# First batch of a fused attention and MLP kernel: K and Q loaded six tokens a row on 96 partitions, strided reads of PSUM, plain key layout, first loads on other queues, the bias table loaded and turned by head pair

## The chip, the cores and the metric

The kernel runs on one core of one Trainium2 chip. The metric is device time in microseconds (us), lower is better. Every experiment ran beside the kernel before on the same chip in the same rounds.

How ratios are computed: a ratio is the mean time of one kernel's runs over the mean time of the runs of the kernel before of the same rounds, with a 95% interval. So it is not quite the ratio of the medians that are quoted beside it.

Engines in the text: PE is TensorE, ACT is ScalarE, DVE is VectorE, POOL is GpSimd, SP is SyncE.

## The reference, cut to what matters

```python
# q, k, v: (8 batches, 8 heads, 576 tokens, 64);  bias_table: (32 buckets, 8 heads)
scores = scale * np.matmul(q, k.transpose(0, 1, 3, 2))
rel = pos[:, None] - pos[None, :]
bucket = ...                                  # a function of |rel|, 32 buckets; far ones are all bucket 31
scores = scores + bias_table[bucket].transpose(2, 0, 1)[None]
attn = exp(scores - max); attn = attn / (sum + 1e-09)
x = (attn @ v)  ->  (4608 tokens, 512)
h = x @ w_in                                  # 512 x 2048
s = np.sin(alpha * h)
out = (h + s * s / (alpha + 1e-09)) @ w_out   # 2048 x 512
```

## The kernel before

The program interleaves batches: while batch t goes through its MLP, the attention of batch t+1 fills the gaps of PE. From about 70 us on that works so well that PE is never free. What is left to gain is the ramp: batch 0's attention, whose K and Q have to be loaded, transposed and copied, and whose position bias has to be built first.

**Scheduling.** A small list scheduler in the program (`plan`) decides at build time on which engine, and in which order, the tasks of PE, ACT and DVE go, from rough durations and from constants such as `T_M2` (the earliest time that it assumes for the bias multiplications). POOL's part, the loads and the bias chain stand in plain program order ahead of it. On the chip each engine then runs its own list strictly in order.

**The bias.** `exp(score + bias)` is computed as `exp(score) * exp(bias)`. The small table `exp(bias)` (8 heads by 512 distances) is made by one matmul (`e_sb`), written to HBM (`e_dram`), read back as 128 shifted rows a head (`m2r`), and turned end for end by POOL (`m2`). For the last 64 keys POOL makes a second form, `mh`, from two slices of `m2`. DVE multiplies bands of the exponentials by `m2` or `mh` before PE multiplies them with V.

```python
    for p in range(NP):                               # NP = 4 pairs of heads
        nc.gpsimd.tensor_copy(
            out=m2[:, 2 * p : 2 * p + 2, :], in_=m2r[:, 2 * p : 2 * p + 2, ::-1]
        )
    me = m2.rearrange("p (hp two) x -> p two hp x", two=2)
    nc.gpsimd.tensor_copy(out=mh[0:64, :, :], in_=me[0:64, 0, :, 0:192])
    nc.gpsimd.tensor_copy(out=mh[64:128, :, :], in_=me[64:128, 1, :, 64:256])
    cast_v(nc.gpsimd, 0)                              # V of batch 0: f32 -> f16, 6 casts
    load_w_in16()                                     # 4 loads, issued by POOL
    for kq, src in ((0, k), (1, q)):
        load_nat(nat2, kq, 0, H, src[1], nc.gpsimd)   # K and Q of batch 1
```

**K and Q of a batch.** Tokens are loaded two to a row (512 bytes), in three loads each, transposed by PE and copied out of PSUM by ACT or DVE. The keys of the odd head are stored with their last 64 ahead of the other 512, which takes an extra small copy.

```python
    SI = 2
    SN = (128, 128, 32)
    SO = (0, 256, 512)
    ...
    def load_nat(dst, kq, h0, h1, src, eng, parts=(0, 1, 2)):
        for j in parts:
            n, o = SN[j], SO[j]
            eng.dma_start(
                out=dst[0:n, j, kq],
                in_=src[h0:h1, o : o + SI * n].rearrange("h (p i) d -> p h (i d)", i=SI),
            )
    ...
        eng = {"DVE": 0.75, "ACT": 0.7}               # the copies: the scheduler may choose
        return [plan.add(eng, cp(x), [m], pri, use=[b]) for x in range(1 if kq else 2)]
```

**Pairs.** Batch 0's attention is done in four pairs of heads (0 to 3), each in two windows of queries (384 and 192). A window ends with an `Ln` on ACT (the softmax denominator's reciprocal is taken as exp(-ln)). So "pair 0's second Ln" marks the end of pair 0's work, and its time is a good mile mark. In a window's order on DVE the multiplication by `mh` belongs to the second window:

```python
                def bh(e):
                    io = u.v[:, 8, 384:576]
                    nc.vector.tensor_tensor(out=io, in0=io, in1=mh[:, p, 0:192], op=ALU.mult)

                x = plan.add({"DVE": 0.17}, bh, [x] + mh_tasks, base + 10, nb=band_nb, use=[ub])
```

The softmax here doesn't subtract the row's maximum and nothing guards it: scores larger than these inputs give would overflow.

## Time and profile before

| | before |
|---|---|
| time, median of 3 runs | 446.3 us (446.24 to 446.53) |
| PE busy, of a span of 445.2 us | 426.2 us (96%) |
| ACT, DVE, POOL busy | 385.3, 261.9, 91.0 us |
| PE busy in the first 50 us | 38.7 us |
| PE busy from 70 to 440 us | 368.0 of 370 us |
| first exp of batch 0 on ACT | 14.70 us |
| pair 0's second Ln | 27.02 us |
| first matmul with w_in (batch 0's MLP begins) | 49.81 us |

PE is idle for 19.0 us of the whole span (445.2 less 426.2), and nearly all of that lies before 70 us or at the very end. So a gain should show as an earlier first matmul with w_in, with everything behind it shifted as a block. (The runs x1, x2 and x10 will show that this mile mark and the time go together only to within 1 to 2 us. The prediction below has 39.7 where the stretches of the trace add up to 38.7; nothing rests on it.)

The table of stretches of the kernel before. Columns: stretch and its length, then busy time (and number of instructions) of PE, weight loads, DVE, ACT, POOL, then PE's mean granted clock (1.00 is full), the busy share of the DMA engines, GB/s.

```profile
core 0: us, PE busy (x) PEld busy (x) DVE busy (x) ACT busy (x) POOL busy (x), PEclk, DMA share, GB/s
15.00:20.00 5.00, 4.60 (x68) 2.92 (x66) 4.49 (x8) 3.57 (x10) 3.67 (x5) 1.00 1.06 239
20.00:25.00 5.00, 2.75 (x41) 1.77 (x38) 3.64 (x7) 4.45 (x12) 4.83 (x9) 1.00 0.31 70
25.00:30.00 5.00, 4.55 (x54) 2.95 (x56) 2.69 (x8) 3.47 (x10) 5.00 (x9) 1.00 1.05 209
30.00:35.00 5.00, 4.70 (x66) 3.57 (x66) 2.25 (x7) 4.97 (x15) 1.22 (x2) 1.00 1.07 205
```

From 30 us ACT is full (4.97 of 5): from there ACT's exponentials set the pace. Before that none of PE, DVE and ACT is full; POOL is, from 20 to 30 us (4.83 and 5.00), and waits set the pace. POOL's timeline of the kernel before says which. Columns: start, duration, engine, line, operation, written and read tile, shapes, count; in brackets the idle time ahead of it and what ended it. (`m2r` shares its memory with `w_out`, so `w_out_80<-e_dram` is the load of `m2r`; `m_77` is `m2`.)

```profile
16.27 3.32 POOL L454 COPY m_77<-w_out_80 128x768 f16<-128x768 f16 x4 [5.81 <-DMA w_out_80<-e_dram]
19.65 1.03 POOL L458 COPY mh<-m_77 64x768 f16<-64x768 f16 x1
20.72 0.93 POOL L459 COPY mh<-m_77 64x768 f16<-64x768 f16 x1
21.71 2.44 POOL L354 CAST v_71<-w_out_80 128x512 f16<-128x512 f32 x4
24.11 0.92 POOL L356 CAST vh_73<-w_out_80 64x256 f16<-64x256 f32 x2
24.98 2.14 POOL L372 DMA_DIRECT2D w_in_79<-in_moe_w_in_dram  x4
```

POOL starts when `m2r` lands (16.27), turns all four pairs, makes all of `mh`, and only then casts V. PE has to wait for that last piece. PE's timeline of the kernel before, the two waits that matter:

```profile
24.61 0.82 PE L388 MATMUL av<-u,vh_73 128*64 128x384 f16 x2 [2.20 <-POOL vh_73 L356]
...
47.81 0.60 PE L501 MATMUL mo<-id_sb,nat_95 128*64 128x128 f16 x8 [1.00 <-DMA nat_95<-in_q_dram]
```

So PE waits 2.20 us for the V cast in pair 0, and 1.00 us for batch 1's Q just before the MLP can begin. ACT's timeline of the kernel before gives the mile marks (first exp; pair 0's second Ln; pair 3's first Ln; the load of the sine table, where ACT turns to the MLP):

```profile
14.70 1.61 ACT L580 ACTIVATE u<-sc 128x384 f16<-128x384 f32 x4
...
27.02 0.33 ACT L662 ACTIVATE lnd<-av 128x192 f32<-128x192 f32 x1 [0.25 <-PE av L646]
...
44.95 0.65 ACT L662 ACTIVATE lnd<-av 128x384 f32<-128x384 f32 x1
...
47.53 1.28 ACT L771 ACT_TABLE_LOAD   x1
```

### The profile page before, as it was taken

The page shows a single profiled execution, that of the slowest core. Times are in us where ns is not written, and L with a number is a line of the kernel's source. Part 1 is how long each engine was busy: PE and PEld are TensorE (multiplying, and loading weights), DVE is VectorE, ACT ScalarE, POOL GpSimd, SP SyncE. Part 2 cuts the span into 40 slices and gives each one's busy share as a digit, 9 for nine tenths or more (in the row PEclk, how much of TensorE's full clock was granted, in tenths as well). Part 3 has the DMA queues.
Part 4 walks back from the last instruction along what each step waited for, and adds up shares of the span by engine and source line. Part 5 has one row for each costly group of instructions (what it writes and reads, how often), then busy time and mean ns, then how long its engine had stood idle before and what let it go on. Part 6 is the DMA issues. An engine that isn't in the chain of part 4 may idle for free.

```text
span 445.2 us, 12071 instructions
## 1 busy us (share of the span) xinstructions
PE 426.2 (96%) x4940; PEld 302.8 (68%) x4940; DVE 261.9 (59%) x555; ACT 385.3 (87%) x844; POOL 91.0 (20%) x104
## 2 busy tenths in 40 slices
PE   5879999999999999999999999999999999999996
PEld 1555545876688668866886688558876787666663
DVE  3646786548655865577457755785568555907400
ACT  2789889999999999999999999999999999936511
POOL 8578931016000700080008000400000000000000
PEclk9999999999999999999999999999999999999999
DMA  9699999909913990099529900981000000011111
GB/s 139 179 183 195 175 168 157 187 29 146 190 38 79 142 151 24 26 127 176 90 37 161 167 31 27 110 138 40 1 26 25 25 26 26 1 49 47 49 72 71
DMA packets 144950, 41.51 MB, mean 93 GB/s; under 512 B 132424, under 2 KB 139776, under 8 KB 144896
## 3 DMA queue, kind: packets, MB, share of 16 engines
q0 software_dynamic: 94720, 16.88, 47.9%
q1 hardware_dynamic: 49360, 23.52, 25.2%
q8 instruction: 38, 0.62, 0.6%
q10 hardware_dynamic: 816, 0.36, 0.4%
q14 instruction: 16, 0.13, 0.1%
HBM read 37.56 MB, written 16.52 MB: 121 GB/s over the span
## 4 chain that ended last, share of the span: by engine, by line
PE 72%; DMA 10%; ACT 10%; DVE 2%; issue 2%; POOL 2%; SPq 1%; ACTq 0%; POOLq 0%; DVEq 0%
PE sc L388 32%; PE mo L388 25%; PE av L646 12%; PE av L388 3%; DMA nat_95<-in_q_dram 3%; DMA w_in_79<-in_moe_w_in_dram 2%; DMA qT_69<-staged_q 2%; ACT L771 2%; ACT sq L716 2%; DVE g L723 1%; DMA w_out_80<-e_dram 1%; DMA tabL<-in_bias_table_dram 1%; POOL m_77 L454 1%; DMA e_dram<-e_sb 1%; ACT u L580 1%
## 5 line engine op out<-in xcount | busy, mean ns | idle before, releaser
L580 ACT ACTIVATE u<-sc 128x384 f16<-128x384 f32 x448 | 175.1, 535 | 1.4 <-PE sc L388 1.3
L388 PE MATMUL mo<-w_out_80,g 128*64 128x512 f16 x1152 | 172.1, 379 | 0.0
L388 PE MATMUL sc<-xT,w_in_79 128*64 128x512 f16 x1152 | 132.6, 379 | 1.0 <-DVE g L723 1.0
L613 DVE TENSOR_TENSOR u<-u,m_77 128x512 f16<-128x512 f16 (+1 forms) x192 | 73.9, 402 | 81.1 <-ACT u L580 81.0
L723 DVE SCALAR_TENSOR_TENSOR g<-sq,inv_a,sc 128x512 f16<-128x512 f16 x144 | 102.2, 744 | 23.9 <-PE mo L388 12.3
L388 PEld LDWEIGHTS <-w_in_79 128*64 128x64 f16 x1152 | 78.0, 110 | 45.4 <-DVE g L723 2.0
L388 PEld LDWEIGHTS <-g 128*64 128x64 f16 x1152 | 79.3, 110 | 22.0
L388 PE MATMUL sc<-qT_70,kz_67 128*64 128x384 f16 (+1 forms) x576 | 68.0, 287 | 2.0 <-ACT u L580 1.1
L388 PE MATMUL sc<-qT_69,kz_66 128*64 128x384 f16 (+1 forms) x576 | 67.1, 292 | 2.3 <-ACT u L580 1.3
L388 PEld LDWEIGHTS <-kz_67 128*64 128x64 f16 x576 | 43.0, 108 | 20.5 <-issue 5.3
L388 PEld LDWEIGHTS <-kz_66 128*64 128x64 f16 x576 | 40.6, 109 | 20.6 <-issue 9.3
L646 PE MATMUL av<-u,ones 128*64 128x192 f16 (+1 forms) x512 | 43.9, 286 | 0.0
L677 DVE TENSOR_TENSOR xT<-av,rd 128x384 f16<-128x384 f32 (+1 forms) x68 | 29.4, 437 | 24.1 <-ACT rd L666 19.9
L479 ACT ACTIVATE outs<-mo 128x512 f32<-128x512 f32 x15 | 8.9, 595 | 30.7 <-PE mo L388 30.7
L646 PEld LDWEIGHTS <-ones 128*64 128x64 f16 x512 | 30.5, 110 | 4.2
L662 ACT ACTIVATE lnd<-av 128x384 f32<-128x384 f32 x64 | 29.3, 458 | 3.4 <-PE av L646 2.9
L335 POOL DMA_DIRECT2D v_72<-in_v_dram x12 | 10.6, 897 | 101.7 <-PE av L646 101.7
L666 ACT ACTIVATE rd<-lnd 128x384 f32<-128x384 f32 x64 | 28.8, 449 | 1.4
L335 POOL DMA_DIRECT2D v_71<-in_v_dram x12 | 11.7, 1215 | 73.0 <-PE av L646 73.0
L646 PE MATMUL av<-u,v_71 128*64 128x384 f16 (+1 forms) x256 | 22.1, 286 | 0.0
L646 PE MATMUL av<-u,v_72 128*64 128x384 f16 (+1 forms) x256 | 21.8, 286 | 0.0
L388 PE MATMUL av<-u,ones_76 128*64 128x192 f16 (+1 forms) x128 | 20.4, 286 | 0.0
(360 smaller groups left out, 413.0 us busy)
## 6 DMA issues: line engine op xcount, KB each, us to landing
out_dram<-outs SPq DMA_DIRECT2D x36, 256.0 KB, 2.0
staged_k<-in_k_dram POOLq DMA_DIRECT2D x6, 576.0 KB, 13.0
staged_q<-in_q_dram POOLq DMA_DIRECT2D x6, 576.0 KB, 17.7
w_out_80<-in_v_dram SPq DMA_DIRECT2D x8, 256.0 KB, 4.9
w_in_79<-in_moe_w_in_dram POOLq DMA_DIRECT2D x4, 512.0 KB, 11.1
w_out_80<-in_moe_w_out_dram POOLq DMA_DIRECT2D x4, 512.0 KB, 9.1
v_71<-in_v_dram POOLq DMA_DIRECT2D x12, 128.0 KB, 7.2
v_72<-in_v_dram POOLq DMA_DIRECT2D x12, 128.0 KB, 7.5
```

The costliest lines, as they stand in the source:

```text
L335: nc.gpsimd.dma_start(out=vs[t % 2][:, c], in_=vp[128 * c : 128 * c + 128],)
L388: nc.tensor.matmul(out=out[64 * z : 64 * z + 64], lhsT=lhsT[:, 64 * z : 64 * z + 64], rhs=rhs, start=start, stop=stop,)
L479: nc.scalar.activation(out=o, in_=i, func=AF.Copy)
L580: nc.scalar.activation(out=u.v[:, k0 : k0 + nc_, q0 : q0 + n], in_=sc.v[:, 0 : n * nc_], func=AF.Exp, scale=0.125,)
L613: nc.vector.tensor_tensor(out=io, in0=io, in1=m2[:, 2 * p : 2 * p + 2, x0 : x0 + hi - lo], op=ALU.mult,)
L646: nc.tensor.matmul(out=o[64 * z : 64 * z + 64, 0:n], lhsT=vs[t % 2][:, c, 2 * p + z, :] if y else ones, rhs=u.v[:, 4 * z + c, q0 : q0 + n] ...
L662: nc.scalar.activation(out=ln.v[:, 0:n], in_=avs[0].v[:, 0:n], func=AF.Ln)
L666: nc.scalar.activation(out=rd.v[:, 0:n], in_=ln.v[:, 0:n], func=AF.Exp, scale=-1.0)
L677: nc.vector.tensor_tensor(out=xT[:, p, (x0 + a) % XN : (x0 + a) % XN + m - a], in0=avs[1].v[:, a:m], in1=rd.v[:, a:m], op=ALU.mult,)
L716: nc.scalar.activation(out=sq.v, in_=s16.v, func=AF.Square)
L723: nc.vector.scalar_tensor_tensor(out=gcell[b].v[:, f, :], in0=sq.v, scalar=inv_a[:, f : f + 1], in1=h.v, op0=ALU.mult, op1=ALU.add,)
L771: nc.scalar.preload_act_table_set(name)
```

## The change

Its intent is to start batch 0 sooner: larger rows in the first loads and fewer of them, no long run of warm-up matmuls ahead of the first transposes, and a bias chain that delivers pair 0's part first. The parts of the diff that matter (cut; `...` marks cuts):

```diff
-T_M2 = 13.0
+T_M2 = 11.0
...
-WARM1 = 6
+WARM1 = 1
...
-    SI = 2
-    SN = (128, 128, 32)
+    SI = 6
+    SN = S // SI                      # 96
...
-    load_nat(nat0, 0, 0, 2, k[0], nc.sync)
+    load_nat(nat0[:, 0], 0, 2, k[0], nc.sync)
     nc.sync.dma_start(out=tabN, in_=bias_table)
...
+    load_nat(nat0[:, 1], 0, 2, q[0], nc.scalar)
+    nc.scalar.dma_start(out=tabL, ...)
...
+    load_v32(0, nc.sync)              # before: behind the load of m2r
...
-    nc.vector.tensor_copy(out=e_sb, in_=eps_[0:H, 0:EW])
-    nc.sync.dma_start(out=e_dram.ap(), in_=e_sb)
+    nc.scalar.activation(out=e_sb, in_=eps_[0:H, 0:EW], func=AF.Copy)
+    nc.scalar.dma_start(out=e_dram.ap(), in_=e_sb)
...
-    nc.sync.dma_start(out=m2r, ...)   # all 8 heads
...
-    for p in range(NP):
-        (reverse pair p of m2r into m2)
+    load_m2r(0, 2)                    # pair 0 alone, issued by POOL
+    for kq, src in ((0, k), (1, q)):
+        load_nat(nat1[:, kq, 2:6], 4, H, src[0], nc.gpsimd)
+    load_m2r(2, H)
+    turn(0)                           # reverse pair 0
+    cast_v(nc.gpsimd, 0)
+    load_w_in16()
+    for p in range(1, NP):
+        turn(p)
     me = m2.rearrange("p (hp two) x -> p two hp x", two=2)
     nc.gpsimd.tensor_copy(out=mh[0:64, :, :], in_=me[0:64, 0, :, 0:192])
     nc.gpsimd.tensor_copy(out=mh[64:128, :, :], in_=me[64:128, 1, :, 64:256])
-    cast_v(nc.gpsimd, 0)
-    load_w_in16()
...
-            pin = c.v[:, 0:S].rearrange("d (i p) -> d i p", i=SI)
+            pin = c.v[:, 0:S].rearrange("d (i p) -> d p i", i=SI)     # read PSUM with a stride
...
-        eng = {"DVE": 0.75, "ACT": 0.7}
+        eng = {"DVE": 0.75, "ACT": 0.72} if kq else {"DVE": 1.6, "ACT": 1.55}
+        if t == 0:
+            eng = {"ACT": 0.72} if p == 0 and kq else {"DVE": eng["DVE"]}
```

The keys lie plainly now (two halves of 576), which drops one small copy a batch. Note POOL's order: the casts of V and the issue of the w_in loads have moved ahead of three of the four reversals and of `mh`. Left out of the cut are smaller moves: the clearing of V's tiles went from POOL to DVE, the first cast of Q from ACT to POOL, the first exponentials of pair 0 come in another order, and the last 64 keys of a pair's two heads are read from two places.

## The prediction

> **What bounds the kernel now.** From 70 to 440 us TensorE is never free: the table of stretches shows PE busy 9.9 to 10.0 of every 10 us, clock 1.00. In the first 50 us it is busy 39.7, about 5 of them warm-up matmuls. So the gain can only come from starting batch 0 sooner; everything after should shift as a block.
>
> By the timeline, the tabL load lands at 7.06; e_sb follows at 8.2 to 8.8, its trip through HBM ends at 11.6, and m2r lands at 16.1. The first k/q transpose waits until 10.75 behind 12 warm-up matmuls; the first exp runs at 14.70. POOL works serially: four m2 reversals (16.27, 3.3 us), mh (2.0), v casts (3.3, to 24.98). The waits show PE waiting 2.2 us for the v cast, so pair 0's second Ln comes only at 27.02. From there to 47.5 ACT is full: 6.6 us for each pair. Then PE waits 1.0 us for batch 1's q (landing 47.8).
>
> **What the change does.**
> - k/q rows of 1536 B rather than 512 B, 1 load for 3, spread over three queues. I estimate tabL and k/q landing about 6, not 7.06: the volume is the same, and the Trainium skill (DMA: Bandwidth & Descriptors, "Issuing engines are not separate DMA queues") says all queues run on the same 16 engines. This trace agrees: the first loads took until about 6.5 us at 139 GB/s.
> - 10 fewer warm-up matmuls after e: transposes at about 7.3, first exp at about 10.3, 4.4 us earlier.
> - K/q copies: about 0.8 us each as now; in batch 0 nearly all move to DVE, which has room from 25 to 40 (2.2 to 2.7 busy of 5 us).
> - m2r split: the first quarter lands at about 14 (e write 2.7 us, load 3 to 4). POOL then does one reversal, the v casts (done about 18, not 25), the w_in issue (2.1), three reversals (2.5), mh (2.1).
>
> **What is lost on the way.** mh now comes last, 0.8+3.3+2.1+2.5+2.1 = 10.8 us after the first m2r lands: about 24.5 to 25, against 21.7 now. DVE's mh multiply (pair 0, second window) stands ahead of the remaining bands, xT and pair 2's copies. I expect DVE idle from about 18 until mh, and pair 0's second Ln at 25 to 26.5 (now 27.02): most of the 4.4 us is lost to mh. After that ACT is full again. Batch 1's q lands well before it is needed (about 35 us), which removes the 1.0 us wait, but ACT now has two kz copies (1.6 us, was 0.8) before its table load. Net: batch 0's MLP starts at about 47, not 49.8. The plain key layout changes no matmul count and drops one small copy per staged batch.
>
> **Predicted: 443.2 us, 8 in 10 between 439.0 and 446.0.** Faster by over 2% (below 437.4): 0.08; within 2%: 0.90; slower by over 2%: 0.02.
>
> **What would show it.** First exp at 9.5 to 11. POOL's mh after 23 us, and DVE waiting several us on mh. Pair 0's second Ln at 25 to 26.5. No PE wait on batch 1's q load. First w_in matmul between 46 and 48.5; the same rates as now from 70 us on.
>
> **What would make it wrong.** The first m2r landing at 12 or earlier: gain 5 us or more. The v loads, now issued early, slowing the bias chain: m2r at 16 and no gain. Strided PSUM reads much slower than 0.8 us, filling DVE. POOL slowed while DVE copies. A schedule change in batch 1 that leaves PE idle before 70 us.

## The result, and the profile after

| | before | after |
|---|---|---|
| time, median of 4 runs of the same rounds | 446.41 us (446.24 to 446.82) | 445.97 us (445.83 to 446.16) |
| ratio, 95% interval | | 0.9989 (0.9972 to 1.0006): the same |
| span of the profiled run; PE busy | 445.2; 426.2 us | 444.2; 423.1 us |
| first exp of batch 0 | 14.70 us | 9.57 us |
| pair 0's second Ln | 27.02 us | 27.43 us |
| pair 3's first Ln | 44.95 us | 46.88 us |
| first matmul with w_in | 49.81 us | 49.83 us |

The kernel after was run twice more as a yardstick, with ratios of 1.0000 and 0.9997. So the 5 us of head start were gone by the end of pair 0, by pair 3 the kernel after was 1.9 us behind, and from there to the MLP it won 1.9 us back (2.95 us, where the kernel before took 4.86). The wait for batch 1's Q, which the kernel before has and the kernel after has not, is 1.00 us of that; the rest was not traced.

The stretches of the kernel after (columns as above):

```profile
15.00:20.00 5.00, 0.65 (x6) 0.37 (x8) 3.38 (x5) 0.41 (x2) 4.71 (x8) 0.79 1.18 270
20.00:25.00 5.00, 3.72 (x24) 1.78 (x20) 0.00 (x0) 2.30 (x5) 4.89 (x8) 0.50 0.98 175
25.00:30.00 5.00, 3.62 (x42) 2.92 (x44) 1.94 (x7) 2.37 (x7) 4.84 (x7) 0.50 1.07 211
30.00:35.00 5.00, 4.35 (x76) 3.46 (x73) 4.89 (x9) 3.93 (x10) 3.47 (x4) 0.85 1.15 195
```

From 15 to 20 us PE worked 0.65 us (4.60 before), from 20 to 25 us DVE did nothing at all (3.64 before), and the only engine that is full from 15 to 30 us is POOL. Also the recorded clock was at half from 17.9 to 31.5 us (and before that from 7.6 to 14.4). In the kernel before it was full from about 17 us on. Its first 17 us were at half clock too, although the column says 1.00 (it says so wherever the trace has no clock record). The times of the matmuls show it. PE's timeline of the kernel before, where the column says 1.00:

```profile
13.91 1.49 PE L388 MATMUL sc<-qT_69,kz_66 128*64 128x384 f16 x8
```

and of the kernel after, where the recorded clock is 0.50; the same eight matmuls take as long:

```profile
27.19 1.49 PE L557 MATMUL sc<-qT,kz 128*64 128x384 f16 x8
```

POOL's timeline of the kernel after:

```profile
10.16 0.74 POOL L394 DMA_DIRECT2D w_out<-e_dram  x1 [2.97 <-DMA e_dram<-e_sb]
...
15.23 0.82 POOL L400 COPY m<-w_out 128x768 f16<-128x768 f16 x1 [2.13 <-DMA w_out<-e_dram]
15.99 2.99 POOL L348 CAST v<-w_out 128x512 f16<-128x512 f32 x4
18.93 0.85 POOL L350 CAST vh<-w_out 64x256 f16<-64x256 f32 x2
19.73 2.16 POOL L361 DMA_DIRECT2D w_in<-in_moe_w_in_dram  x4
21.93 2.36 POOL L400 COPY m<-w_out 128x768 f16<-128x768 f16 x3
24.35 0.82 POOL L449 COPY mh<-m 64x768 f16<-64x768 f16 x1
25.21 0.82 POOL L450 COPY mh<-m 64x768 f16<-64x768 f16 x1
```

`mh` ends at 26.03 (25.21 + 0.82); before it ended at 21.65. DVE's timeline of the kernel after shows who wants it:

```profile
16.08 2.42 DVE L598 TENSOR_TENSOR u<-u,m 128x512 f16<-128x512 f16 x3 [3.23 <-POOL m L400]
18.54 0.76 DVE L470 COPY qT<-mo 128x576 f16<-128x576 f16 x1
19.21 0.28 DVE L598 TENSOR_TENSOR u<-u,m 128x256 f16<-128x256 f16 x1
26.07 0.26 DVE L581 TENSOR_TENSOR u<-u,mh 128x192 f16<-128x192 f16 x1 [6.58 <-POOL mh L450]
```

DVE stands idle for 6.58 us in front of one multiplication of 0.26 us, while other work that it could do stands behind it in its list. And a smaller thing: pair 1's copy of Q (the `qT` line, 0.76 us) stands behind three bands that wait for `m2`. PE waits for both, as its timeline of the kernel after shows:

```profile
19.35 0.85 PE L557 MATMUL sc<-qT,kz 128*64 128x384 f16 x4 [4.61 <-DVE qT L470]
...
26.38 0.37 PE L377 MATMUL av<-u,ones 128*64 128x192 f16 x2 [2.66 <-DVE u L581]
```

No wait for batch 1's Q is left on PE. ACT's mile marks of the kernel after:

```profile
9.57 3.33 ACT L565 ACTIVATE u<-sc 128x384 f16<-128x384 f32 x8 [0.62 <-PE sc L557]
...
27.43 0.33 ACT L647 ACTIVATE lnd<-av 128x192 f32<-128x192 f32 x1 [3.18 <-PE av L631]
...
46.88 0.64 ACT L647 ACTIVATE lnd<-av 128x384 f32<-128x384 f32 x1
```

### The profile page after: what moved, and what is told of

The parts are those of the page before. It is cut to its first block, busy times and chain, and to the rows that moved or that the text cites. A ratio compares the mean times of both kernels' runs of the same rounds, so it can differ in the third digit from the quotient of the medians.

```text
span 444.2 us, 12031 instructions
## 1 busy us (share of the span) xinstructions
PE 423.1 (95%) x4934; PEld 306.1 (69%) x4934; DVE 262.4 (59%) x554; ACT 382.9 (86%) x834; POOL 84.5 (19%) x95
## 4 chain that ended last, share of the span: by engine, by line
PE 71%; ACT 16%; issue 3%; DVE 3%; DMA 3%; POOL 2%; ACTq 0%; DVEq 0%; POOLq 0%
PE mo L377 24%; PE sc L377 18%; PE sc L557 14%; PE av L631 12%; ACT s L694 6%; ACT u L565 4%; PE av L377 3%; ACT L756 2%; ACT sq L701 2%; DVE g L708 1%; DMA w_out<-e_dram 1%; DMA tabL<-in_bias_table_dram 1%; DVE kz L470 1%; ACT rd L651 1%; ACT lnd L647 1%
## 5 line engine op out<-in xcount | busy, mean ns | idle before, releaser
L377 PE MATMUL mo<-w_out,g 128*64 128x512 f16 x1152 | 172.2, 379 | 0.0
L557 PE MATMUL sc<-qT,kz 128*64 128x192 f16 (+1 forms) x1152 | 134.8, 296 | 8.8 <-DVE qT L470 5.3
L377 PE MATMUL sc<-xT,w_in 128*64 128x512 f16 x1152 | 132.7, 379 | 1.3 <-DVE g L708 1.3
L598 DVE TENSOR_TENSOR u<-u,m 128x512 f16<-128x512 f16 (+1 forms) x192 | 73.5, 400 | 72.1 <-ACT u L565 68.6
L557 PEld LDWEIGHTS <-kz 128*64 128x64 f16 x1152 | 84.7, 112 | 42.8 <-issue 10.6
L377 PEld LDWEIGHTS <-w_in 128*64 128x64 f16 x1152 | 80.3, 110 | 44.1 <-issue 2.8
L694 ACT ACTIVATE s<-sc,alphaT 128x512 f16<-128x512 f32 x144 | 92.5, 678 | 3.5 <-PE sc L377 2.5
L701 ACT ACTIVATE sq<-s 128x512 f16<-128x512 f16 x75 | 47.2, 629 | 2.3
L631 PE MATMUL av<-u,v 128*64 128x192 f16 (+1 forms) x512 | 44.7, 291 | 0.0
L631 PEld LDWEIGHTS <-v 128*64 128x64 f16 x512 | 30.7, 112 | 3.9
```

The costliest lines, as they stand in the source:

```text
L377: nc.tensor.matmul(out=out[64 * z : 64 * z + 64], lhsT=lhsT[:, 64 * z : 64 * z + 64], rhs=rhs, start=start, stop=stop,)
L557: nc.tensor.matmul(out=sc.v[64 * g : 64 * g + 64, n * y : n * y + n], lhsT=kzs[t % 2][:, p, k0 : k0 + 64], rhs=qTs[t % 2][:, p, q0 : q0 + ...
L598: nc.vector.tensor_tensor(out=io, in0=io, in1=m2[:, 2 * p : 2 * p + 2, x0 : x0 + hi - lo], op=ALU.mult,)
L631: nc.tensor.matmul(out=o[64 * z : 64 * z + 64, 0:n], lhsT=vs[t % 2][:, c, 2 * p + z, :] if y else ones, rhs=u.v[:, 4 * z + c, q0 : q0 + n] ...
L694: nc.scalar.activation(out=s16.v, in_=h.v, func=AF.Sin, scale=alphaT[:, f : f + 1])
L701: nc.scalar.activation(out=sq.v, in_=s16.v, func=AF.Square)
```

## The experiments

The theories:

- **A**: POOL's serial order makes `mh` late, and DVE, which works in order, passes the delay on to PE and ACT. A lesser part of it is DVE's own order (pair 1's Q copy behind the bands).
- **B**: DVE is overloaded, since it now has nearly all copies of batch 0.
- **C**: the half-speed clock of PE between 20 and 30 us, which follows its idle time, costs what is lost.
- **D**: the loads of V, now early, slow the bias chain.

All eighteen runs gave correct results. Unless said otherwise an edit is to the kernel after.

### x1_warm6: give the head start back

```diff
-WARM1 = 1
+WARM1 = 6
```

> The changed kernel with six warm-up pairs after the e matmul in place of one (10 more matmuls, 2.1 us, on TensorE only; the bias chain goes on beside them). Theory A (the early head is off the chain, because POOL's work on m2 and mh decides when pair 0 ends): first exp about 2 us later (11.6 instead of 9.57), mh still done at about 26.0, pair 0's second Ln still at 27.4 within 0.3, time within 0.4 us of the changed kernel (445.9). Rival B (the head start is worth what it saves, and the loss is made later, for example by DVE or the clock): 1.5 to 2.1 us slower, about 447.8.

Measured: 446.67 us, ratio 0.9984 (0.9964 to 1.0004). The first exp came at 11.48 instead of 9.57, `mh` ended at 26.8, pair 0's second Ln came at 28.23. The time did not suffer: to within about 1 us, the width of the intervals, two microseconds of head start are worth nothing here, since pair 0 ends when `mh` does. (That the profiled run's MLP began at 50.63, 0.8 us later than in the kernel after, did not show in the time.)

### x2_gapwarm: a longer run of idle matmuls in PE's first gap

```diff
-    plan.warm = lambda: warm(1)
+    plan.warm = lambda: warm(9)
```

> The changed kernel with the one pair of filler matmuls that stands ahead of TensorE's 4.6 us wait (14.7 to 19.3) made nine pairs, so that TensorE stays busy there; no other engine's order changes. Rival C (TensorE's clock, which the records show at 0.50 from 20 to 30 us, eats the gain): granted clock about 1.0 from 20 to 35, attention matmuls of pair 0 and 1 at half their time, pair 0's second Ln 0.5 to 1 us earlier, time 1 to 2 us lower (444 to 445). Theory A (POOL's order decides): the clock may rise, but Ln at 27 still, because mh is only there at 26.0; gain at most 0.7 us.

Measured: 446.75 us, ratio 0.9991 (0.9971 to 1.0011). No gain, but the test was weak: the granted clock was still 0.66 from 20 to 25 us and 0.78 from 25 to 30 us. Theory C was left open by it and taken up again below (x13, x17).

### x3_mh0 and x15_mh0_again: pair 0's quarter of mh directly behind its reversal

```diff
+    me = m2.rearrange("p (hp two) x -> p two hp x", two=2)
     turn(0)
+    nc.gpsimd.tensor_copy(out=mh[0:64, 0:1, :], in_=me[0:64, 0, 0:1, 0:192])
+    nc.gpsimd.tensor_copy(out=mh[64:128, 0:1, :], in_=me[64:128, 1, 0:1, 64:256])
     cast_v(nc.gpsimd, 0)
     load_w_in16()
     for p in range(1, NP):
         turn(p)
-    (all four quarters of mh)
+    (the other three quarters of mh)
```

> The changed kernel with mh split by head pair: pair 0's quarter is made right after the first reversal, the other three quarters where mh was. Theory A: DVE's 6.6 us wait on mh goes; pair 0's second Ln comes at 23 to 24 instead of 27.43, pair 1 meets its own mh wait at about 26.5, and the first w_in matmul moves from 49.8 to about 47, time 443 within 1. Rival B or C (DVE load from the copies moved there, or the clock): Ln earlier, but the first w_in matmul still at 49 to 50 and the time within 0.7 us of 445.9.

> The single move of pair 0's quarter of mh once more: ratio 0.988 to 0.992, second Ln of pair 0 at about 24 us, if the earlier 0.9897 was not luck of one chip.

Measured: 442.36 us, ratio 0.9897 (0.9875 to 0.9920), and again on another chip 442.49 us, ratio 0.9912 (0.9888 to 0.9936). This is the one edit that brings what the change was to bring. POOL's timeline of the first run:

```profile
15.55 0.82 POOL L400 COPY m<-w_out 128x768 f16<-128x768 f16 x1 [1.86 <-DMA w_out<-e_dram]
16.44 0.60 POOL L445 COPY mh<-m 64x192 f16<-64x192 f16 x1
17.08 0.58 POOL L446 COPY mh<-m 64x192 f16<-64x192 f16 x1
17.72 2.44 POOL L348 CAST v<-w_out 128x512 f16<-128x512 f32 x4
```

and DVE's timeline of the same run, in which the multiplication by `mh` has no wait in brackets any more:

```profile
18.64 0.47 DVE L600 TENSOR_TENSOR u<-u,m 128x256 f16<-128x256 f16 x1
19.03 0.66 DVE L583 TENSOR_TENSOR u<-u,mh 128x192 f16<-128x192 f16 x1
19.61 1.16 DVE L600 TENSOR_TENSOR u<-u,m 128x256 f16<-128x256 f16 x2
```

Pair 0's second Ln came at 24.05 (27.43 in the kernel after), and the first matmul with w_in at 46.63 (49.83): 3.2 us earlier, and by the ratios the run is 4.1 us faster than the kernel after (0.9989 less 0.9897, of 446.4), though of different rounds. Theory A holds. The single copies also show a price of company: 0.60 and 0.58 us for 64 x 192 elements, while DVE multiplies.

### x4_qfirst: pair 1's Q copy ahead of the bands on DVE

```diff
-T_M2 = 11.0
+T_M2 = 13.0
```

> The changed kernel with the planner's earliest time for band multiplies at 13 instead of 11, so that on DVE the copy of pair 1's q comes ahead of pair 0's band multiplies (which wait for m2). Takes away TensorE's 4.6 us wait and with it the clock drop; mh stays late. Theory A: first exps of pair 1 run at 14 to 17 instead of 19.9, no PE gap before 19, but pair 0's second Ln stays at about 27 since mh is done at 26.0; ACT has done four more exps by then, so the gain is 1 to 2 us (444 to 445). Rival C (clock): gain 2 us or more. Rival B (DVE load): no gain.

Measured: 444.59 us, ratio 0.9947 (0.9923 to 0.9971). PE's wait of 4.6 us for pair 1's Q is gone, and twenty exps run back to back from 10.26 us. Yet DVE still waits 7.0 us for `mh`, and pair 0's second Ln is no earlier (28.09). The first matmul with w_in came at 48.95. So DVE's order is a cost of its own, of the lesser size: 0.9 us in the mile mark, 1.9 us by the ratios (0.9989 less 0.9947, of 446.4, of different rounds).

### x5_before_order: the kernel before, with the change's order on POOL alone

This edit is to the kernel before:

```diff
-    for p in range(NP):
+    for p in range(0, 1):
         (reverse pair p)
+    cast_v(nc.gpsimd, 0)
+    load_w_in16()
+    for p in range(1, NP):
+        (reverse pair p)
     (mh)
-    cast_v(nc.gpsimd, 0)
-    load_w_in16()
```

> The kernel before with one part of the change alone: POOL's order of the change (one reversal, v casts, w_in issue, three reversals, mh); loads, copies, queues and everything else as before. Theory A (POOL's order with mh last decides when pair 0 ends): mh done at about 27.1 (16.3+0.8+3.3+2.1+2.5+2.1) where it was 21.7, DVE waits some us on mh, pair 0's second Ln at 28.5 to 29 instead of 27.02, 1 to 2 us slower than before. Rival B (the loss lies in the copies moved to DVE): no slower than before, or faster, because v is ready at 20.5 instead of 25.

Measured: 449.98 us, ratio 1.0067 (1.0047 to 1.0087): the order alone makes the old kernel 2.6 us slower than its companion at 447.36. DVE's timeline of this run has the same wait, even longer:

```profile
28.72 0.26 DVE L600 TENSOR_TENSOR u<-u,mh 128x192 f16<-128x192 f16 x1 [8.03 <-POOL mh L465]
```

That is the harm of the order, measured without any other part of the change.

### x6_before_pool: the kernel before, with POOL's order mended

Also an edit to the kernel before: reverse pair 0, make pair 0's quarter of `mh`, cast V, reverse the rest, make the rest of `mh`, issue w_in.

```diff
-    for p in range(NP):
+    for p in range(0, 1):
         (reverse pair p)
-    (all four quarters of mh)
+    (pair 0's quarter of mh)
     cast_v(nc.gpsimd, 0)
+    for p in range(1, NP):
+        (reverse pair p)
+    (the other three quarters of mh)
     load_w_in16()
```

> The kernel before with POOL's order mended: one reversal, pair 0's quarter of mh, v casts, three reversals, the rest of mh, then w_in as before. Theory A: v ready at about 21.6 instead of 25, pair 0's second Ln at about 24 instead of 27.02. But w_in and batch 1's k/q loads are issued no earlier and still land at about 48, so the TensorE wait on batch 1's q grows from 1.0 to 2 to 4 us, and of the 3 us only 0 to 1 reach the end: 445.5 to 446.9. If instead 3 us reach the end (about 443.5), the change's larger loads have no part in the gain.

Measured: 444.96 us, ratio 0.9957 (0.9935 to 0.9979), pair 0's second Ln at 25.18 (27.02), first matmul with w_in at 47.62 (49.81). I had expected at most 1 us, since PE's wait for batch 1's Q was to grow to 2 to 4 us; that wait was 0.68 us, and the edit brought 1.9 us by the ratio (0.43% of 447.36). So the kernel before too was held up by POOL in pair 0: its order there had the V casts last.

### x7_v_late: the loads of V behind the bias chain again

```diff
-    load_v32(0, nc.sync)
...
-    nc.scalar.dma_start(out=e_dram.ap(), in_=e_sb)
+    nc.sync.dma_start(out=e_dram.ap(), in_=e_sb)
+    load_v32(0, nc.sync)
```

> The changed kernel with the write of e moved to the sync queue and batch 0's v loads queued behind it, as in the kernel before, so that they start after 7.6 instead of at about 3. Tests whether the early v loads (1.2 MB in 256-byte rows) slow the bias chain. If they do: the first m2r quarter lands at 13.5 to 14.3 instead of 15.2 to 16, mh follows 1 to 1.5 us earlier, and the time drops by as much. If not: m2r at 15 to 16, and v casts may even wait for their loads; time equal or up to 1 us slower.

Measured: 452.27 us, ratio 1.0111 (1.0090 to 1.0132). The first quarter of `m2r` landed no sooner (15.27, against 15.23), while POOL's cast of V's last piece waited 4.07 us for its load, and everything behind it, `mh` included, came 4 us later (DVE waited 10.5 us for it). Theory D falls as the cause of the loss: the early loads are needed. They are not shown to be harmless. With them out of the way (and the write on SP's queue) the trip of `e` to HBM took 1.56 us (7.70 to 9.26) instead of 2.56 (7.60 to 10.16); but then they ran beside the first quarter of `m2r`, which took 5.9 us to land instead of 4.9. No run keeps them clear of both.

### x8_both: x3 and x4 together

```diff
-T_M2 = 11.0
+T_M2 = 13.0
...
(and the edit of x3_mh0)
```

> The changed kernel with both mends: pair 0's quarter of mh made right after the first reversal, and pair 1's q copy ahead of pair 0's band multiplies. Theory A: no PE wait of 4 us on q, no DVE wait on pair 0's mh; pair 0's second Ln at 21 to 22 with four more exps done by then, pair 1 waits for its own reversal and mh (24 to 27.5). First w_in matmul at 44 to 46 unless batch 1's q, which lands at 42 to 46, holds it. Time 440.5 to 442.5, 0 to 1.5 us below the mh mend alone (442.4). If batch 1's q load is the next limit, the PE wait on it is 1 to 3 us and the gain over the mh mend is under 0.7 us.

Measured: median 443.94 us (442.31 to 444.39), ratio 0.9929 (0.9909 to 0.9950). Its profiled run (442.31) is the fastest of the six and began the MLP at 45.76, earlier than x3; four of the others lie between 443.9 and 444.4. Such a spread of some 2 us shows in x3, x14, x15 and x18 too (x14: five runs from 440.99 to 441.54 and one of 444.34), and in the kernel before (446.09 to 448.98 in the rounds of x1 to x4); what it comes from was not found. The mean clock listed for each execution doesn't go with it (x15: 441.67 and 443.71, both at 0.992). A gap of that size is seen at 90 us in x12 below; whether such gaps come and go was not tested, as only one execution of a run is traced. In any case the two parts don't add up: DVE now waits 3.72 us for pair 1's reversal, which stands behind the issue of w_in on POOL. Mending one item of a serial list brings up the next.

### x9_after_again: the kernel after, as a yardstick

> The changed kernel itself once more, five rounds, on the same chip as the three runs beside it, so that they can be compared with it directly. Expected: 0.998 to 1.000 of the kernel before, mh done at 26 to 27, first w_in matmul at 49.5 to 51.

Measured: 446.58 us, ratio 1.0000 (0.9983 to 1.0016). The trace repeats: `mh` to 26.06, pair 0's second Ln at 27.46, first matmul with w_in at 49.86.

### x10_act_copies: K and Q copies of batch 0 on either engine

```diff
-        if t == 0:
-            eng = {"ACT": 0.72} if p == 0 and kq else {"DVE": eng["DVE"]}
```

> The changed kernel with one part undone: in batch 0 the copies of the transposed K and Q may again go to either engine, as in the kernel before (three q copies and two K pairs go to the scalar engine, DVE is relieved of about 4 us). Rival B (DVE load by the moved copies took the gain): 2 to 3 us faster than the changed kernel. Theory A (mh last): mh still done at 26, pair 0's second Ln still at 27 to 28, time within 1 us of the changed kernel.

Measured: 446.12 us, ratio 0.9991 (0.9977 to 1.0005). With copies moved to ACT, DVE waits 7.0 us for `mh` all the same, and nothing changes in the time. Theory B falls: up to `mh` DVE is not short of time, it stands still. (The MLP of this run began at 51.45, 1.6 us later than in the kernel after, and the time doesn't show it: so a shift of this mile mark by 1 to 2 us is not yet a gain or a loss. In the kernel after PE still has 1.5 us of idle time between 50 and 70 us, which may be where it goes.)

### x11_m2r_alone: nothing queued behind the first quarter of m2r

```diff
     load_m2r(0, 2)
+    turn(0)
+    (pair 0's quarter of mh)
     (loads of nat1[2:6])
     load_m2r(2, H)
-    turn(0)
     cast_v(nc.gpsimd, 0)
     ...
+    (the other three quarters of mh at the end, as in x3)
```

> The mh mend (pair 0's quarter of mh early) with the other loads of POOL's queue (the rest of batch 0's k and q, the rest of m2r) issued after the first reversal and not before it. Tests the mis-sized term, m2r's first quarter landing at 15.2 to 16 where 14 was expected: if those loads behind it in the same queue slow it, it lands at 13.5 to 14.5 and the time drops by 1 us or more below the mh mend; if it is slow by itself (or by the v loads), it still lands at 15 to 16, and the time is equal or up to 2 us worse, because the rest of m2r and pair 2's rows then come later.

Measured: 443.37 us, ratio 0.9931 (0.9917 to 0.9946). By the list of DMA issues the first quarter landed 3.5 us after its issue (issued at 10.89, POOL goes on at 14.57), while it takes 4.9 us in the kernel after (10.16, 15.23) and 4.6 us in x3, which issued it at nearly the same time as x11 (10.76). In the other runs with this order of loads it takes 4.6 to 5.9 us. So 1.1 to 1.4 us of it, by one trace, are due to the three loads (288, 288 and 576 KB) that POOL queues right behind it. But the loads behind it then come later, the other reversals wait (0.93 us), and the sum is no better than x3.

### x12_best and x14_inter_q: each pair's mh behind its own reversal

```diff
-T_M2 = 11.0
+T_M2 = 13.0
...
     turn(0)
+    make_mh(0)
     cast_v(nc.gpsimd, 0)
+    turn(1)
+    make_mh(1)
     load_w_in16()
-    for p in range(1, NP):
+    for p in range(2, NP):
         turn(p)
-    (mh)
+        make_mh(p)
```

x12 also put batch 1's V loads on POOL's queue, behind batch 1's K and Q (`load_v32(1, nc.gpsimd)` for `load_v32(1, nc.sync)`); x14 did not.

> The changed kernel with the waits that the runs showed taken away in turn: each pair's quarter of mh made right after its reversal, pair 1's reversal and mh ahead of the w_in issue, pair 1's q copy ahead of pair 0's band multiplies, and batch 1's v loads queued behind batch 1's k and q. Theory A with batch 1's q as the next limit: pair 1's m2 ready at about 21.5 (23.7 with both mends), batch 1's q landing by 42, first w_in matmul at 43.5 to 45.5, time 440 to 442.5, that is 0.985 to 0.990 of the kernel before. If the limit has moved elsewhere, no better than the mh mend alone (0.9897).

> Each pair's quarter of mh directly behind its reversal, pair 1's before the w_in issue, pair 1's q copy ahead of the bands on DVE; batch 1's v loads where the kernel after has them. If the earlier combined version lost only to its delayed v loads, this one is at least as fast as the single move of pair 0's mh: ratio 0.985 to 0.990, first w_in matmul at about 45 us. If something else costs it (order of fill work between the stages), it is again at 0.993, with the first w_in matmul early all the same.

Measured: x12 443.61 us, ratio 0.9933 (0.9916 to 0.9950); x14 441.31 us, ratio 0.9896 (0.9866 to 0.9925). Both begin the MLP at 45.3 and 45.05 us, yet x12 lost it again 45 us later. Its stretch around 90 us, and then that of x14:

```profile
90.00:95.00 5.00, 2.57 (x35) 1.85 (x32) 1.63 (x4) 1.83 (x6) 0.00 (x0) 1.00 0.78 174
```

```profile
90.00:95.00 5.00, 5.00 (x66) 3.87 (x64) 1.66 (x5) 4.08 (x9) 1.86 (x3) 1.00 0.78 168
```

PE lost 2.4 us there (2.57 against 5.00). In x12 the later V casts of batch 1 pushed POOL's issue of the staging copies of later batches from 41.79 to 51.15 us; DVE then waited 3.8 us for an output tile to be stored, at 85 to 100 us. That the delayed V loads are the cause is shown by taking them back: x14 has no such gap. It is the fastest kernel seen here by its median, but its ratio is not distinguishable from that of x3 and x15.

### x13_clock and x17_clock_again: hold PE's clock up

Idle matmuls in both gaps of PE:

```diff
-    plan.warm = lambda: warm(1)
+    plan.warm = lambda: warm(13)
...
             def mm(e, y=y):
+                if t == 0 and p == 0 and w == 1 and not y:
+                    warm(6)
```

> The kernel after, with idle matmuls in both gaps of TensorE (between 14.7 and 19.3 us and between 23.7 and 26.4 us), so that the granted clock stays near 1.0 through 20 to 30 us. If the serial order on POOL and DVE sets the pace (theory A), the time stays within 0.7 us of the kernel after, and mh still ends at about 26.0 and the second Ln of pair 0 at about 27.4. If the lowered clock costs what was lost after mh (rival C), the first Ln of pairs 1 to 3 comes 1 to 2 us earlier and the time falls by 1 to 2 us, ratio about 0.996.

> The clock run again. If the half-speed clock costs part of what was lost after mh, it is 0.8 to 1.5 us faster than the kernel after on the same chip; if it is only a shift in the trace that is paid back later, within 0.4 us of it.

Measured: 445.13 us, ratio 0.9971 (0.9950 to 0.9992), and again 445.68 us, ratio 0.9977 (0.9956 to 0.9998). Stretches of the second run:

```profile
15.00:20.00 5.00, 3.00 (x30) 1.69 (x28) 3.38 (x5) 0.93 (x3) 4.72 (x8) 0.97 1.17 257
20.00:25.00 5.00, 4.62 (x34) 2.40 (x30) 0.00 (x0) 2.12 (x5) 4.89 (x8) 0.69 1.04 197
25.00:30.00 5.00, 3.47 (x66) 2.69 (x67) 3.21 (x9) 2.83 (x9) 4.84 (x7) 1.00 1.07 212
```

The clock is full from 25 us on in both runs. As theory A says, `mh` ends at 26.0 and pair 0's second Ln stays (27.29 and 27.18). But then pair 1's first Ln comes at 33.35 and 33.24 instead of 34.51, and the first matmul with w_in at 48.63 and 48.53 instead of 49.83: 1.2 to 1.3 us. So theory C seems true of a part, the part behind `mh`; in the time it is less sure, as the next run shows.

### x16_after_third: the kernel after on the same chip as x17 and x18

> The kernel after a third time, as the yardstick of this chip: ratio 0.998 to 1.001 to the kernel before, granted clock 0.50 from 20 to 30 us.

Measured: 446.60 us, ratio 0.9997 (0.9977 to 1.0017). Against it x17 is 0.9 us faster by the medians. The intervals of the two ratios overlap, so in the time this is a likely size, not a proven one; in the traces both clock runs show it at the same place. (In this run the clock was 0.59 from 20 to 25 us and 0.75 from 25 to 30, so it was not as low as in the first profile of the same kernel.)

### x18_mh0_clock: x3 with the first gap of PE filled

```diff
-    plan.warm = lambda: warm(1)
+    plan.warm = lambda: warm(15)
(and the edit of x3_mh0)
```

> Pair 0's quarter of mh behind its reversal, and idle matmuls in the gap of TensorE from 14.6 to 18.2 us, so that its clock stays near 1.0 until 30 us. If serial order and clock are separate costs, they add up: ratio 0.986 to 0.988, first w_in matmul about 45.5 us (46.6 with mh alone), second Ln of pair 0 still at about 23.5 to 24. If the clock only mattered because mh was late, the time equals that of the move alone, ratio 0.990 to 0.991.

Measured: 444.28 us, ratio 0.9932 (0.9911 to 0.9952). No sum of gains: it is, if anything, slower than x3 and x15 (0.9897, 0.9912), and its fastest run, 442.49, is not below theirs (441.87, 441.67) either. The clock was full from 12 to 29 us and pair 0's second Ln came at 21.95, which is 1.6 us earlier than in x15. Then PE, too, came to stand before DVE. PE's timeline of this run:

```profile
26.89 0.45 PE L489 MATMUL mo<-id_sb,nat 96*64 96x96 f16 x12 [1.44 <-DVE kz L472]
28.14 0.52 PE L559 MATMUL sc<-qT,kz 128*64 128x384 f16 x4 [0.80 <-DVE qT L472]
```

DVE's copies came when they came in x15 too (to within 0.4 us), for they stand behind a band of pair 1 that needs POOL's second reversal. (In x15 the trace names that reversal as what DVE waits for; in x18 it names an exp of ACT, but the band starts at 23.29, within 0.05 us of the reversal's end, so the two came together.) So PE ran ahead, waited, lost its clock (half from 29.1 to 32.5 us) and ended pair 1 at 32.90 instead of 31.63. In these runs the clock was worth something only where the others waited for PE.

## Why the prediction was right or wrong

**Right.**

- *The class, and the mechanism.* "Most of the 4.4 us is lost to mh" is what happened; the head start was 5.1 us, and all of it was lost. x3 and x5 show it from both sides: the order on POOL costs the old kernel 0.67%, and moving a single quarter of `mh` makes the new one 0.9 to 1.0% faster than before. The rest of the change is worth about what the order takes: on the same POOL order, after against before is 0.9989 / 1.0067 = 0.992, an estimate from two ratios of different rounds (the two kernels don't load `m2r` in the same pieces). Nearly equal and opposite parts: that is why the sum is nil.
- *First exp at 9.5 to 11*: 9.57. *POOL's mh after 23 us*: 24.35 to 26.03. *DVE waiting several us on mh*: 6.58. *No PE wait on batch 1's q*: none. *About 0.8 us for a strided copy out of PSUM*: 0.76 for Q. *The same rates from 70 us on*: PE was busy 367.7 of 370 us from 70 to 440 us, against 368.0.
- *All queues run on the same 16 engines.* The Trainium skill (DMA: Bandwidth & Descriptors, "Issuing engines are not separate DMA queues") says that moving loads to other queues saves only issue time. The trace agrees as far as it goes: the last row of the bias table, now issued by ACT at 1.20 us instead of by SP at 3.19, took longer than before (4.6 us instead of 3.9), so its earlier landing is time of issue. The two loads of 288 KB, on two queues, landed after 4.4 and 4.6 us. No run separates rows from queues, and the 139 GB/s that the prediction names (the page's mean over the first 11 us) don't show which engines carried them.

**Wrong: the size of the gain**, 3.2 us (446.4 less 443.2) predicted, 0.44 us measured. In short: the prediction placed the end of `mh` 1.0 to 1.5 us too early (24.5 to 25, measured 26.03), and took ACT as full from then on, which it was not until about 35 us. The failed steps, as the prediction put them:

1. *"The first quarter lands at about 14 (e write 2.7 us, load 3 to 4)."* The write was about right (7.60 to 10.16). The load took 4.9 us, not 3 to 4, and landed at about 15.2. By x11, 1.1 to 1.4 us of it come from the loads that POOL queues right behind it; alone it took 3.5 us. The rule of the Trainium skill (DMA: Bandwidth & Descriptors, "Anatomy of one DMA"), 2.0 us plus the bytes at 436 GB/s, would give an estimate of 2.5 us for these 192 KB; the measured 3.5 us alone and 4.9 us in company decide against it.
2. *mh "about 24.5 to 25"; "pair 0's second Ln at 25 to 26.5."* The chain of 10.8 us on POOL was right in its sum (15.23 to 26.03 is 10.8), with some luck: the casts of V took 3.7 us instead of 3.3, and `mh` 1.7 instead of 2.1. Hung on a later start it ended at 26.03, and the second Ln at 27.43. So the term "net gain in pair 0", about 1.3 us in the prediction (27.02 less its middle, 25.75), was -0.4 us.
3. *"After that ACT is full again."* This failed outright. Of the 2.8 us by which the MLP began later than predicted (49.83 against 47), 1.7 us were there at pair 0's second Ln (27.43 against 25.75), so steps 1 and 2 are the larger part, and 1.1 us came after it. (From pair 0's second Ln to pair 3's first this step lost 1.5 us against the kernel before, but part was won back before the MLP: step 4.) Between 25 and 30 us ACT was busy 2.37 of 5 us, between 30 and 35 us 3.93, where it had 3.47 and 4.97 before. Pair 1's first Ln came 2.7 us later than before (34.51 against 31.78), pair 3's 1.9 us. What the runs put in its place: about 1.2 us in the mile marks go with PE's half-speed clock (x13, x17), which the prediction did not consider although it foresaw DVE idle until `mh`. Another part is the order on DVE, with pair 1's Q copy behind the bands: PE waited 4.6 us for it, and x4 shows 0.9 us of it in the MLP's start. These parts overlap, since that very wait is one of the gaps that lower the clock, so they can't be added. How the rest divides among DVE's pent-up work was not separated.
4. *"batch 0's MLP starts at about 47, not 49.8."* It started at 49.83. The removed wait for batch 1's Q (1.00 us) was real, but it went into paying back the loss in step 3 rather than adding a gain.

**Rivals.** B (DVE overloaded) and D (early V loads in the way) were each tried and fell: x10 changed nothing, and x7 made it worse (though it freed `e`'s trip of 1.0 us). C is likely true for about a microsecond. About the clock, the Trainium skill (TensorE: Matmul & The Clock Gate, "What's actually happening") says that half rate is the default, that an idle window of some 3.4 us brings it back, and that about as long of work lifts it. The traces agree with the first two: the kernel before started at half clock (1.49 us for the eight matmuls at 13.91); in the kernel after the clock fell at 17.9 us, in PE's gap of 4.6 us (14.7 to 19.35), while in the kernel before, in the gap of 2.2 us ahead of 24.61, it stayed 1.00. The lift varied: in x17 PE worked from 19.35 and the clock was full from 23.1 us (3.8 us); in x13 PE was busy from 19.48 without a break and the mean clock of 20 to 25 us was 0.50, so there it took over 5 us. The page does add that its window runs freely and that the moment varies.

**What stays open.** The spread of some 2 us within the runs of several kernels has no explanation here, and the MLP's start and the time part by up to 1.6 us (x10). The part of the loss between 27 and 35 us that is neither clock nor the Q copy is not separated. That the clock is worth 0.9 us in the time, and not only in the trace, is likely and not proven. And the separate worth of larger rows, of other queues and of fewer warm-up matmuls was not measured; x1 shows only that in this kernel, with `mh` late, giving up 2 us of head start cost nothing that could be seen.

## What to carry to other kernels

When a chain is started sooner, list for each in-order engine what stands ahead of the *last* item that the first consumer needs, and give it only its own piece first: here a quarter of `mh`, two copies of 0.6 us, decided over 4 us. A split that delivers one tile early is worth nothing if a sibling tile of the same consumer is left at the end of the list. And where an engine is to idle for several microseconds in the ramp, count its slower work afterwards too, but repair the wait first: filling the gap helped by about 1 us where the wait remained (likely, not proven in the time), and by nothing that showed where the wait was mended.

## What the Trainium skill lacked or had wrong

- DMA: Bandwidth & Descriptors, "Anatomy of one DMA": the rule gives an estimate of 2.5 us for a load of 192 KB issued by POOL. Here, reading 768-byte rows from HBM, it took 3.5 us alone (x11) and 4.9 us with three loads of 288, 288 and 576 KB queued behind it by the same engine (after). That loads issued *later* on the same queue slow an earlier one is missing.
- TensorE: Matmul & The Clock Gate, "What's actually happening": about 3.4 us of work are said to lift the clock, with a moment that varies. In x17 it took 3.8 us, in x13 over 5 us (0.50 over 20 to 25 us, in work unbroken since 19.5 us), and in the kernel after, where a second gap of 2.7 us followed 4.4 us of work, the clock stayed at half until 31.5 us. What a short gap costs that falls before the clock has come back is missing.
- SBUF — State Buffer, "Who interferes with whom": it says that a DVE instruction with two inputs in SBUF contends with a POOL instruction that reads SBUF. The traces agree, and give the size: a POOL copy of 64 x 192 took 0.60 us beside DVE's multiplications (x3, x14) and 0.34 us while DVE worked out of PSUM (x14), and DVE's multiplication by `mh` took 0.66 us beside POOL's cast of V (x3), 0.26 us with no POOL copy or cast beside it (after). The page speaks of a full block of one instruction, and has no such figures for short instructions in a row.
- DMA: Bandwidth & Descriptors, "Issuing engines are not separate DMA queues": the time that an engine takes to initiate a DMA is called usually small beside the DMA. Beside each load that holds here too (0.54 us, against a median of 8.8 us from issue to landing). What is missing is its cost on an engine that also computes: on POOL the issue of the four loads of w_in took 2.16 us of the 10.8 us chain that decided over pair 0 (after).
